# Three of eight chunks loaded transposed, and four stages of a kernel's written-out order moved by a half step

## The chip, the cores and the metric

The kernel runs on one core of one Trainium2 chip. The metric is the device time of one execution in microseconds; three runs before the change gave 368.6, 368.87 and 369.53 us, and their median, 368.87 us, is the time before.

## What is computed

For 2048 rows of 448 columns the kernel adds three things: the input, a gated long convolution, and a two-layer network with the Mish activation. Both branches take the layer-normalised input.

```python
xn = _layernorm(A_q)                                   # over the 448 columns, eps 1e-5
k_shift = sum(k_pad[:, t:t+S] * shift_k[:, 3-t] for t in range(4))
kv = k_shift * v
y = irfft(rfft(kv, 4096) * rfft(ssm_k, 4096))[:S] + kv * ssm_D
h = xn @ w1 + b1                                       # 448 -> 1792
out = A_q + xn * y + (h * tanh(softplus(h))) @ w2      # 1792 -> 448
```

## The kernel before

**The network** sets the skeleton. The rows are cut into 8 chunks of 256 (two tiles of 128, called jj), the 1792 hidden columns into 7 pairs p of 2 x 128. The program is a list of 116 slots, that is half steps, written out by `mlp_slot`: pair i = 7c + p has its first matmul stage (`g1_mm`, 22 matmuls with 256 columns) in slot 2i, its activation (`mish`) in slot 2i + 1, and its second matmul stage (`g2_mm`, 12 matmuls with 448 columns) two pairs later, in slot 2(i + 2) + 1. Every float32 operand is split in a rounded high part and a low part (XH and XL, ach and acl, w1h and w1l, w2h and w2l), and products high x high, high x low and low x high are added up.

**The layer norm** of chunk c + 1 is made while chunk c is worked on. `ln_load` brings 256 rows with rows on partitions; `bn_stats` and `bn_aggr` on DVE make mean and variance of each row, POOL makes rstd, and (x - mean) * rstd is one instruction for 128 rows on POOL (on DVE for chunks 0 and 7). DVE's share of it is put in a list (`drip`), of which `dv()` pops one entry between other DVE instructions. `g1_mm` needs the columns on partitions, so `ln_T` lets TensorE transpose each 128-row tile in four 128 x 128 blocks against an identity matrix: tile 0 in slot 14c - 3, tile 1 in slot 14c - 2, for chunk c whose first `g1_mm` is in slot 14c. The block of columns 384 to 447 is stored twice (`tail` copies 64 columns), because the fourth block carries a high and a low part in its two halves. ACT copies the transposed block out of PSUM as XH (L419), DVE subtracts for XL (L417). For chunks 5 to 7 these two are put off to the end of the slot's matmuls (`turned`, `T_LATE`).

**The convolution** is a Fourier transform in stages that are threaded through the same slots. Groups of the kernel h and of kv = (shifted k) * v are transformed by 16 packed matmuls (`f1_mm`, L125), folded on ACT and DVE (`f1_fold`) and stored to HBM scratch by DMAs from ACT's queue (`f1_out`, to Dh and Dkv, L140). `H_AT` names the slot of each h group, `KV_AT` that of each kv group; the store follows three slots later and the load five slots before. `taps` makes kv on DVE, with one product of four on POOL (`taps_pool`). From slot 63 on eight octets are read back (`o_load`: ah and av) and transformed (`h2_mm`, `v2_mm`, `prod`, `i1_mm`), and from slot 98 on `i2_mm` and `gate` finish chunk by chunk.

**What sets the order**: `at(slot, f)` puts f before the slot's network work, `after(slot, f)` behind it, and within one slot the calls run in the order in which they were registered. Each engine, and each of the DMA queues of SP, ACT and POOL, works through its own instructions in that order. Buffers: w1 and w2 pieces and k tiles share four `kr` buffers, h, v and tap tiles share seven `x` buffers, the q tiles of the chunks share three `qt` buffers, and there is one `xn`.

**The output**: `g2_evac` adds a chunk's result to its q tile, and for chunks 0 to 5 SP stores the tile at once (L494) in slot 14c + 18; the gated convolution is added to it in HBM later.

Of the kernel before, what the change touches and what calls it, by code (L numbers as in the profile page):

```python
# [7 lines left out]
F32 = mybir.dt.float32  # L8
# [7 lines left out]
NJ = 16  # L16
# [21 lines left out]
@with_exitstack  # L38
def tile_kernel(ctx: ExitStack, tc, q, k, v, sk, hT, sD, w1, b1, w2, c_f1, c_g, c_gi, c_i2, out):
    nc = tc.nc  # L40
# [24 lines left out]
    rstd = cp.tile([128, NJ], F32, name="rstd")  # L65


    w1h = wp.tile([128, 4, F], F32R, name="w1h")
# [49 lines left out]
    def f1_mm(src, g, key):  # L118
        x = src.pop(g)
        PS[key, g] = ps = [pc(), pc()]  # L120
        for b in range(2):
            for h in range(2):
                for jj in range(2):
                    rg = 32 * (2 * b + h)
                    nc.tensor.matmul(ps[h][64 * jj:64 * jj + 64, b, :D], f1[rg:rg + 32, 0:64], x[rg:rg + 32, jj],  # L125
                                     start=True, stop=True, tile_position=(rg, 64 * jj))
# [185 lines left out]
    def gate(c):  # L312
        p = PS.pop(("P", c))
        for jj in range(2):
            j = 2 * c + jj
            r = rstd[:, j:j + 1]
# [43 lines left out]

    XS, XN, turned = {}, {}, []

    def ln_load(c, eng=None):
# [3 lines left out]
        else:  # L367
            for jj in range(2):
                nc.sync.dma_start(Q[c][:, jj], q[:, jj])

    def ln_parts(c):
        st = mp.tile([128, 2, 6], F32, name="bst", bufs=2)
        ve = mp.tile([128, 2], F32, name="ve", bufs=2)
        xn = mp.tile([128, 2, D + 64], F32, name="xn", tag="xn", bufs=1)
        XN[c] = xn
        eng = nc.gpsimd if 0 < c < NCHUNK - 1 else V

        def stats(jj):
            V.bn_stats(st[:, jj], Q[c][:, jj])

        def aggr(jj):
            V.bn_aggr(mv[:, 2 * c + jj], st[:, jj])

        def eps(a, b):
            V.tensor_scalar(ve[:, a:b], mv[:, 2 * c + a:2 * c + b, 1], EPS, None, op0=ALU.add)  # L385

        def power(a, b):
            nc.gpsimd.tensor_tensor(rstd[:, 2 * c + a:2 * c + b], ve[:, a:b], mhalf[:, a:b], op=ALU.pow)  # L388

        def norm(jj):  # L390
            j = 2 * c + jj
            eng.tensor_scalar(xn[:, jj, :D], Q[c][:, jj], mv[:, j, 0:1], rstd[:, j:j + 1],  # L392
                              op0=ALU.subtract, op1=ALU.mult)

        def tail(a, b):
            eng.tensor_copy(xn[:, a:b, D:], xn[:, a:b, D - 64:D])
# [24 lines left out]
    def ln_T(c, jj):  # L421
        if jj == 0:
            dv(len(drip))
            x_tiles(c)
        p = g1p.tile([128, 2, CH], F32, name="pg1").rearrange("p a b -> p (a b)")
        transposes(c, jj, p)

        def halves():
            for lo in range(2):
                x_split(c, jj, p, lo)  # L430

        turned.append(halves)
        if c < T_LATE:
            turn()

    def turn():
        while turned:
            turned.pop()()

# [46 lines left out]
    def g2_evac(c, jjs=(0, 1)):  # L486
        x = Q[c]
        for jj in jjs:
            V.tensor_add(x[:, jj], P2.pop((c, jj))[:, :D], x[:, jj])
            dv()  # L490
            if late(c):
                nc.sync.dma_start(out[:, 2 * c + jj], x[:, jj])
        if not late(c):
            nc.sync.dma_start(out[:, 2 * c:2 * c + 2], x)  # L494

    def mlp_slot(s):
# [3 lines left out]
        if half == 0:  # L500
            if i < n:
                c, p = pairs[i]
                if c + 1 < NCHUNK:
                    if p == 0:
                        ln_load(c + 1)
                    if p == (3 if c in (0, 2, NCHUNK - 2) else 2):
                        ln_stats(c + 1)
                    if c == 0:
                        dv(len(drip))
                    if p == NP - 1:  # L510
                        ln_T(c + 1, 1)
                g1_mm(i)
        else:
            if i < n:
                c, p = pairs[i]
                if p == NP - 2 and c + 1 < NCHUNK:
                    ln_T(c + 1, 0)
# [26 lines left out]
    for g, t in enumerate(KV_AT):  # L544
# [8 lines left out]
        after(t, f1_fold, g, "kv")  # L553
        at(t + 3, f1_out, Dkv, g, "kv")

# [39 lines left out]
    wz = cp.tile([128, NJ], F32, name="wz")  # L595
    V.memset(wz, 0.0)
    ve0 = cp.tile([128, 2], F32, name="ve0")
    warm = g2p.tile([128, 512], F32, name="pg2")
    for _ in range(WARM):
        nc.tensor.matmul(warm[0:NJ, 0:WARM_N], wz, wz[:, 0:1].to_broadcast([128, WARM_N]), start=True, stop=True)  # L600

# [35 lines left out]
    for s in range(nslots):  # L637
# [7 lines left out]
        for fn, args in fns:  # L645
            if fn in (h2_out, v2_out, i1_out):
                fn(*args)
        turn()
        for fn, args in fns:
# [6 lines left out]
def _constants():  # L656
# [19 lines left out]
    for kk in range(64):  # L676
# [8 lines left out]
    c = lambda a: np.ascontiguousarray(a, dtype=np.float32)  # L685
    return dict(c_f1=c(np.stack([f1, np.eye(128)], axis=1)), c_g=c(G.reshape(128, 8, 4, 2, 32)), c_gi=c(GI.reshape(128, 8, 2, 2, 64)),
                c_i2=c(i2))
# [27 lines left out]
```

## Time and profile before

| what | value |
|---|---|
| median of 3 runs | 368.87 us |
| the profiled execution's own time | 370.86 us |
| its span from first to last instruction | 368.9 us |
| TensorE clock granted | full, in all 40 slices |
| DVE busy | 262.5 us, 71% |
| ACT busy | 166.3 us, 45% |
| POOL busy | 71.2 us, 19% |
| moved by DMA | 79.35 MB |

The span and the 1.96 us around it make up the profiled execution. PE stands for TensorE's matmuls, PEld for its weight loads, DVE for VectorE, ACT for ScalarE, POOL for GpSimd; SPq, ACTq and POOLq are the queues from which these engines issue DMAs. A row of the timeline has start and duration in us, engine, line, operation, tiles written and read, shapes, a count, and in brackets the idle time before it with what ended it. Several matmuls are in flight at once, so the distance from one start to the next is a matmul's cost, and its duration is not.

### The profile page before, as it was taken

How to read it: one execution, taken by the hardware profiler on the slowest of the kernel's cores; microseconds unless marked ns; L12 is line 12 of the kernel's file. 1: busy time of each engine (PE TensorE's matmuls, PEld its weight loads, DVE VectorE, ACT ScalarE, POOL GpSimd, SP SyncE). 2: the span in 40 equal slices, each digit the busy share in tenths (PEclk: the TensorE clock that was granted, in tenths of full speed). 3: DMA queues.
4: the chain of work that ended last, by engine and by line, in shares of the span. 5: the costliest groups of instructions: out<-in, count | busy, mean ns of one | idle time of the engine just before them, and what ended most of it. 6: DMA issues, size and time to landing. Idle time of an engine off the chain costs nothing.

```text
span 368.9 us, 7464 instructions
## 1 busy us (share of the span) xinstructions
PE 360.9 (98%) x3128; PEld 292.6 (79%) x3128; DVE 262.5 (71%) x359; ACT 166.3 (45%) x277; POOL 71.2 (19%) x58
## 2 busy tenths in 40 slices
PE   7998999999999999999999999999999999999995
PEld 2697888978888989889868666666666889889885
DVE  5897858999998888996515657656385752897751
ACT  3757543344241443253254555556655533235450
POOL 2005000920228222611006000060000005102020
PEclk9999999999999999999999999999999999999999
DMA  7998996839496329514675598896694375949655
GB/s 241 346 285 312 358 368 184 256 105 295 105 299 214 89 66 274 170 48 101 225 244 174 194 261 238 282 301 189 209 292 125 95 248 205 419 195 276 116 66 133
DMA packets 32354, 79.35 MB, mean 215 GB/s; under 512 B 2881, under 2 KB 19138, under 8 KB 32322
## 3 DMA queue, kind: packets, MB, share of 16 engines
q1 hardware_dynamic: 20210, 44.09, 35.8%
q10 hardware_dynamic: 9776, 22.88, 22.2%
q0 software_dynamic: 2336, 11.93, 11.3%
q8 instruction: 24, 0.39, 0.4%
q14 instruction: 8, 0.07, 0.1%
HBM read 50.44 MB, written 28.44 MB: 214 GB/s over the span
## 4 chain that ended last, share of the span: by engine, by line
PE 71%; DMA 12%; DVE 9%; POOL 3%; ACT 2%; issue 2%; SPq 0%; ACTq 0%; POOLq 0%; DVEq 0%
PE pg L457 27%; PE pg L482 10%; PE pg L484 9%; PE pg L483 9%; PE pc L208 7%; DMA kr<-in_w_dram 6%; PE pc L251 4%; PE pc L125 2%; PE pc L308 2%; DMA Dh<-st 2%; DVE x L172 2%; PE pg L407 2%; POOL xn L392 2%; DMA Dkv<-st 1%; DMA av<-Dkv 1%
## 5 line engine op out<-in xcount | busy, mean ns | idle before, releaser
L465 ACT ACTIVATE a<-pg,b1t 128x256 f32<-128x256 f32 x112 | 47.1, 472 | 113.0 <-PE pg L457 88.2
L457 PE MATMUL pg<-XH,w1h 128*128 128x256 f32 x448 | 91.3, 285 | 0.9 <-ACT XH L419 0.9
L75 DVE TENSOR_TENSOR acl<-a,ach 128x512 fp32r<-128x512 f32 x56 | 38.8, 693 | 65.0 <-ACT ach L74 64.7
L457 PEld LDWEIGHTS pg<-XH,w1h 128*128 128x128 f32 x448 | 69.6, 188 | 18.9 <-issue 15.7
L482 PE MATMUL pg<-w2h,ach 128*128 128x448 f32 x224 | 83.1, 371 | 0.0
L483 PE MATMUL pg<-w2l,ach 128*128 128x448 f32 x224 | 81.3, 363 | 0.9 <-DVE w2l L75 0.9
L484 PE MATMUL pg<-w2h,acl 128*128 128x448 f32 x224 | 81.4, 363 | 0.0
L457 PE MATMUL pg<-XL,w1h 128*128 128x256 f32 x448 | 69.6, 277 | 0.2 <-DVE XL L417 0.2
L457 PEld LDWEIGHTS pg<-XL,w1h 128*128 128x128 f32 x448 | 59.4, 188 | 0.4 <-DVE XL L417 0.4
L457 PE MATMUL pg<-XH,w1l 128*128 128x256 f32 x336 | 56.8, 277 | 0.0
L482 PEld LDWEIGHTS pg<-w2h,ach 128*128 128x128 f32 x224 | 42.0, 188 | 11.7 <-issue 9.4
L457 PEld LDWEIGHTS pg<-XH,w1l 128*128 128x128 f32 x336 | 46.8, 188 | 0.0
L483 PEld LDWEIGHTS pg<-w2l,ach 128*128 128x128 f32 x224 | 42.1, 188 | 3.6 <-DVE w2l L75 1.2
L484 PEld LDWEIGHTS pg<-w2h,acl 128*128 128x128 f32 x224 | 42.1, 188 | 2.5
L388 POOL TENSOR_TENSOR rstd<-ve,mhalf 128x2 f32<-128x2 f32 (+1 forms) x9 | 8.8, 977 | 156.2 <-DVE ve L385 156.1
L74 ACT CAST ach<-a 128x512 fp32r<-128x512 f32 x56 | 34.7, 620 | 1.8
L155 POOL TENSOR_TENSOR x<-kr,skb 128x896 f32<-128x896 f32 x8 | 17.1, 2133 | 83.6 <-DVE x L154 62.4
L392 POOL TENSOR_SCALAR xn<-qt,mv,rstd 128x448 f32<-128x448 f32 x12 | 27.8, 2320 | 0.6
L172 DVE TENSOR_TENSOR x<-x 128x896 f32<-128x896 f32 x24 | 26.8, 1115 | 1.4 <-POOL x L155 0.9
L131 ACT COPY st<-pc 128x896 f32<-128x896 f32 x16 | 14.5, 906 | 14.5 <-PE pc L125 12.6
L132 DVE TENSOR_TENSOR st<-pc,st 128x896 f32<-128x896 f32 x16 | 17.4, 1088 | 3.6 <-ACT st L131 3.1
L259 ACT COPY qe<-pc 128x896 f32<-128x896 f32 x16 | 13.8, 912 | 11.0 <-PE pc L251 10.8
(70 smaller groups left out, 389.7 us busy)
## 6 DMA issues: line engine op xcount, KB each, us to landing
Dh<-st ACTq DMA_DIRECT2D x16, 448.0 KB, 6.4
Dkv<-st ACTq DMA_DIRECT2D x16, 448.0 KB, 5.1
ah<-Dh SPq DMA_DIRECT2D x8, 896.0 KB, 7.0
av<-Dkv SPq DMA_DIRECT2D x8, 896.0 KB, 6.2
E<-qe ACTq DMA_DIRECT2D x16, 448.0 KB, 5.2
e<-E POOLq DMA_DIRECT2D x8, 896.0 KB, 7.9
kr<-in_k_dram SPq DMA_DIRECT2D x10, 448.0 KB, 6.7
x<-in_v_dram SPq DMA_DIRECT2D x8, 448.0 KB, 5.2
```

What stands on the lines that cost most here:

```text
L74: nc.scalar.copy(h, raw)
L75: V.tensor_sub(l, raw, h)
L132: V.tensor_add(st[:, 0], e, st[:, 1])
L155: nc.gpsimd.tensor_mul(o, KR[g - u // 2], skb[:, u:u + 1].to_broadcast([128, 2, D]))
L172: V.tensor_add(KV[g], KV[g], o)
L208: nc.tensor.matmul(p[32 * t:32 * t + 32, r, :D], g[rs, t, c], a[rs, t], start=True, stop=True, tile_position=(64 * r, 32 * t))
L392: eng.tensor_scalar(xn[:, jj, :D], Q[c][:, jj], mv[:, j, 0:1], rstd[:, j:j + 1], op0=ALU.subtract, op1=ALU.mult)
L457: nc.tensor.matmul(ps[:, n], l, r, start=n_ == 0, stop=n_ == len(mm) - 1)
L465: nc.scalar.activation(a[:, n], ps[:, n], AF.Mish, bias=b1t[:, 2 * p + n:2 * p + n + 1])
L482: nc.tensor.matmul(ps, ah[:, n, cs], w2h[:, f], start=f == 0, stop=False)
L483: nc.tensor.matmul(ps, ah[:, n, cs], w2l[:, f], start=False, stop=False)
L484: nc.tensor.matmul(ps, al[:, n, cs], w2h[:, f], start=False, stop=f == NF - 1)
```

## The change

For chunks 5, 6 and 7 (`NT = 5`) the host supplies q a second time, already transposed (`qT`: 128 partitions, four column blocks, 256 rows, the last block repeated in part). It is loaded straight into the `xn` buffer. Mean and variance still come from the rows-on-partitions tile. Since each row now is a column, mean and rstd have to be the same on all partitions: POOL stores the 256 pairs (mean, rstd) to a scratch row in HBM (`nt_store`), SP reads half of that row back to all 128 partitions (`nt_row`, once for each jj), and DVE subtracts and multiplies in place (`nt_norm`, two instructions with 512 elements a partition for each jj). ACT and DVE then make XH and XL from SBUF (`nt_split`). The tile for the row takes over the identity matrix's space. No transposes are made for these chunks. The slots are written relative to b = 14(c - 1).

Besides: h groups 3, 0, 4 and 5, their loads and stores move one slot later, and `POOL_H` from 20 to 21. The output stores of chunks 0 to 5 move to the end of the slot after. For chunks 1 to 4 the `tail` copy of tile 0 runs before the norm of tile 1. The last kv store moves from slot 63 to 62, the first octet's ah load from the start of slot 61 to the end of slot 60. The constants f1 and identity become two loads, f1 (half as wide) last in ACT's first loads.

```diff
-H_AT = {2: 4, 3: 8, 0: 12, 4: 16, 5: 20, 6: 26, 7: 32}
+H_AT = {2: 4, 3: 9, 0: 13, 4: 17, 5: 21, 6: 26, 7: 32}
-POOL_H = {20: (0, 2)}
+POOL_H = {21: (0, 2)}
-T_LATE = 5
+NT = 5
+NT_AT = {"q": -5, "x": -1, "stats": -2, "flush": 0, "row": (4, 8), "norm": (7, 10), "split": (8, 11)}
...
+    MR = {c: dp.tile([2, CH], F32, name="MR") for c in range(NT, NCHUNK)}
-    f1id = cp.tile([128, 2, 128], F32, name="f1id")
-    f1, ident = f1id[:, 0], f1id[:, 1]
+    f1 = cp.tile([128, 64], F32, name="f1")
+    idr = cp.tile([128, CH], F32, name="idr")
+    ident = idr[:, 0:128]
...
-                     lambda: [f(*a) for f, *a in ((power, 0, 2), (norm, 0), (norm, 1), (tail, 0, 2))]])
+                     lambda: [f(*a) for f, *a in ((power, 0, 2), (norm, 0), (tail, 0, 1), (norm, 1), (tail, 1, 2))]])
+
+    def xT_load(c):
+        XN[c] = xn_tile()
+        nc.sync.dma_start(XN[c], qT[c])
+
+    def nt_stats(c):
+        stats, aggr, eps, power, norm, tail = ln_parts(c)
+        drip.extend([lambda: stats(0), lambda: stats(1), lambda: aggr(0), lambda: aggr(1),
+                     lambda: (eps(0, 2), power(0, 2), nt_store(c))])
+
+    def nt_store(c):
+        nc.gpsimd.dma_start(MR[c].rearrange("j (p t) -> p j t", t=2), mv[:, 2 * c:2 * c + 2])
+
+    def nt_row(c, jj):
+        nc.sync.dma_start(idr, MR[c][jj].partition_broadcast(128))
+
+    def nt_norm(c, jj):
+        x = XN[c][:, :, 128 * jj:128 * jj + 128]
+        for t, op in enumerate((ALU.subtract, ALU.mult)):
+            m = idr.rearrange("p (a t) -> p t a", t=2)[:, t:t + 1].to_broadcast([128, 4, 128])
+            V.tensor_tensor(x, x, m, op=op)
+            dv()
+
+    def nt_split(c, jj):
+        if jj == 0:
+            x_tiles(c)
+        x, h, l = (t[:, :, 128 * jj:128 * jj + 128] for t in (XN[c], *XS[c]))
+        nc.scalar.copy(h, x)
+        V.tensor_sub(l, x, h)
+        dv()
...
-        if not late(c):
-            nc.sync.dma_start(out[:, 2 * c:2 * c + 2], x)
+
+    def g2_out(c):
+        nc.sync.dma_start(out[:, 2 * c:2 * c + 2], Q[c])
...
-        at(t + 3, f1_out, Dkv, g, "kv")
+        at(t + (3 if g < NO - 1 else 2), f1_out, Dkv, g, "kv")
...
-        at(h - d if o else h - 2, o_load, AH, Dh, o, "ah")
+        (at if o else after)(h - d if o else h - 3, o_load, AH, Dh, o, "ah")
...
+    for c in range(NT, NCHUNK):
+        b = 2 * NP * (c - 1)
+        at(b + NT_AT["q"], ln_load, c)
+        at(b + NT_AT["x"], xT_load, c)
+        at(b + NT_AT["stats"], nt_stats, c)
+        at(b + NT_AT["flush"], lambda: dv(len(drip)))
+        for jj in range(2):
+            at(b + NT_AT["row"][jj], nt_row, c, jj)
+            after(b + NT_AT["norm"][jj], nt_norm, c, jj)
+            after(b + NT_AT["split"][jj], nt_split, c, jj)
...
+    for c in range(NCHUNK - LATE):
+        after(2 * (NP * (c + 1) + G2_LAG) + 1, g2_out, c)
...
-    nc.scalar.dma_start(f1id, c_f1)
+    nc.scalar.dma_start(ident, c_id)
...
+    nc.scalar.dma_start(f1, c_f1)
```

More of the change, by code (lines that the diff above doesn't have):

```diff
@@ L38, in tile_kernel @@
 @with_exitstack
-def tile_kernel(ctx: ExitStack, tc, q, k, v, sk, hT, sD, w1, b1, w2, c_f1, c_g, c_gi, c_i2, out):
+def tile_kernel(ctx: ExitStack, tc, q, qT, k, v, sk, hT, sD, w1, b1, w2, c_f1, c_id, c_g, c_gi, c_i2, out):
     nc = tc.nc
@@ L65, in tile_kernel, with rs @@
     rstd = cp.tile([128, NJ], F32, name="rstd")
+    def rs(c):
+        return rstd[:, 2 * c:2 * c + 2] if c < NT else mv[:, 2 * c:2 * c + 2, 1]
     w1h = wp.tile([128, 4, F], F32R, name="w1h")
@@ L315, in gate @@
             j = 2 * c + jj
[L316 removed]
+            r = rs(c)[:, jj:jj + 1]
             x = (Q if late(c) else QA)[c][:, jj]
@@ L369, in ln_load, with xn_tile @@
                 nc.sync.dma_start(Q[c][:, jj], q[:, jj])
+    def xn_tile():
+        return mp.tile([128, 4, CH], F32, name="xn", bufs=1)
     def ln_parts(c):
@@ L373, in ln_parts @@
         ve = mp.tile([128, 2], F32, name="ve", bufs=2)
-        xn = mp.tile([128, 2, D + 64], F32, name="xn", tag="xn", bufs=1)
-        XN[c] = xn
+        if c < NT:
+            XN[c] = xn = xn_tile().rearrange("p a b -> p (a b)").rearrange("p (j d) -> p j d", j=2)
         eng = nc.gpsimd if 0 < c < NCHUNK - 1 else V
@@ L426, in ln_T @@
         transposes(c, jj, p)
[L428 to L438, printed above, removed]
+        for lo in range(2):
+            x_split(c, jj, p, lo)
     AHL, P1, P2 = {}, {}, {}
@@ L502, in mlp_slot @@
                 c, p = pairs[i]
-                if c + 1 < NCHUNK:
+                if c + 1 < NT:
                     if p == 0:
                         ln_load(c + 1)
-                    if p == (3 if c in (0, 2, NCHUNK - 2) else 2):
+                    if p == (3 if c in (0, 2) else 2):
                         ln_stats(c + 1)
@@ L515, in mlp_slot @@
                 c, p = pairs[i]
-                if p == NP - 2 and c + 1 < NCHUNK:
+                if p == NP - 2 and c + 1 < NT:
                     ln_T(c + 1, 0)
@@ L594, in tile_kernel @@
     V.memset(one, 1.0)
-    wz = cp.tile([128, NJ], F32, name="wz")
+    wz = cp.tile([128, 8], F32, name="wz")
     V.memset(wz, 0.0)
@@ L599, in tile_kernel @@
     for _ in range(WARM):
-        nc.tensor.matmul(warm[0:NJ, 0:WARM_N], wz, wz[:, 0:1].to_broadcast([128, WARM_N]), start=True, stop=True)
+        nc.tensor.matmul(warm[0:8, 0:WARM_N], wz, wz[:, 0:1].to_broadcast([128, WARM_N]), start=True, stop=True)
     nc.scalar.activation(ve0, mhalf, AF.Mish)
@@ L696 @@
     lay = lambda x: x.reshape(32, 2, 2, 16, D).transpose(2, 1, 0, 3, 4).reshape(128, NJ, D)
+    rows = np.concatenate([np.arange(D), np.arange(384, D)]).reshape(4, 128)
+    turn = lambda x: x.reshape(128, NCHUNK, 2, D)[..., rows].transpose(1, 4, 3, 2, 0).reshape(NCHUNK, 128, 4, CH)
     kpad = np.pad(a["A_k"][0], ((4, 0), (0, 0)))
     arrs = dict(
-        q=lay(a["A_q"][0]), k=np.concatenate([lay(kpad[:S])[:, :, :][:, :4], lay(a["A_k"][0])], axis=1),
+        q=lay(a["A_q"][0]), qT=turn(lay(a["A_q"][0])), k=np.concatenate([lay(kpad[:S])[:, :, :][:, :4], lay(a["A_k"][0])], axis=1),
         v=lay(a["A_v"][0]), sk=a["A_shift_k"].T, hT=lay(a["A_ssm_k"].T), sD=a["A_ssm_D"][None],
```

11 lines of the change are left out of this document (5 added, 6 removed).

## The prediction

> **What bounds the kernel now.** First the page's busy line and the windows, to see which engine fills which stage.
>
> ```profile
> PE 360.9 (98%) x3128; PEld 292.6 (79%) x3128; DVE 262.5 (71%) x359; ACT 166.3 (45%) x277; POOL 71.2 (19%) x58
> ```
>
> ```profile
> 30.00:40.00 10.00, 9.06 (x62) 8.39 (x61) 9.12 (x12) 7.79 (x13) 3.77 (x3) 1.00 0.89 299
> 60.00:80.00 20.00, 20.00 (x155) 17.46 (x154) 18.57 (x28) 8.05 (x15) 10.99 (x6) 1.00 0.70 209
> 80.00:100.00 20.00, 20.00 (x166) 16.72 (x165) 19.57 (x27) 7.61 (x14) 2.14 (x1) 1.00 0.63 184
> 100.00:120.00 20.00, 19.71 (x156) 17.16 (x155) 18.85 (x27) 5.70 (x11) 9.91 (x5) 1.00 0.81 257
> 180.00:200.00 20.00, 19.66 (x196) 15.47 (x195) 7.00 (x11) 8.61 (x17) 5.83 (x4) 1.00 0.76 251
> 220.00:240.00 20.00, 20.00 (x234) 12.82 (x233) 12.50 (x16) 10.39 (x15) 0.00 (x0) 1.00 0.87 266
> ```
>
> Columns are the stretch, its length, then busy us of PE, PEld, DVE, ACT and POOL, the granted clock (1.00 throughout), DMA share and GB/s. PE is full except in three windows. So the time is TensorE's own work plus a few short stalls, and a cut pays in full only if it shortens PE's sequence or one of those stalls. From 60 to 120 us DVE is a second bound: 57 of 60 us busy. After 180 us DVE has room (7.5 us idle of 20 at 220 to 240).
>
> Then the timeline, for the three stalls. At 31 us:
>
> ```profile
> 31.45 0.47 PE L482 MATMUL pg<-w2h,ach 128*128 128x448 f32 x1
> 32.87 0.47 PE L483 MATMUL pg<-w2l,ach 128*128 128x448 f32 x1 [0.94 <-DVE w2l L75]
> 33.18 0.36 PE L484 MATMUL pg<-w2h,acl 128*128 128x448 f32 x1
> 33.38 0.36 PE L482 MATMUL pg<-w2h,ach 128*128 128x448 f32 x1
> ```
>
> Undisturbed 448-column matmuls start 0.20 apart (33.18 to 33.38); this pair is 1.42 apart, so 1.2 us are lost. The chain of waits tells why:
>
> ```profile
> 20.06 8.35 DMA kr<-in_w_dram
> 28.44 0.58 ACTq L140
> ...
> 31.43 1.39 DVE w2l L75
> 32.87 0.47 PE pg L483
> ```
>
> ACT's queue stood at the issue of an h store (L140) until a w2 load had landed, though the store does not read that tile. Behind it ACT's activation and the split of w2 came late. I infer that the two transfers share a completion semaphore.
>
> At 118 us and 191 us:
>
> ```profile
> 118.39 0.55 PE L407 MATMUL pg<-f1id,xn 128*128 128x128 f32 x3
> 119.23 0.33 PE L407 MATMUL pg<-f1id,xn 128*128 128x128 f32 x1 [0.29 <-POOL xn L396]
> 119.31 0.45 PE L482 MATMUL pg<-w2h,ach 128*128 128x448 f32 x1
> ```
>
> ```profile
> 112.89 5.69 POOL xn L392 x2
> 118.64 0.55 POOL xn L396
> ```
>
> ```profile
> 191.70 1.33 PE L208 MATMUL pc<-av,g 64*32 64x448 f32 x20 [0.34 <-DMA av<-Dkv]
> ```
>
> Chunk 3's transposes wait for a tail copy that stands behind both norms on POOL (2.85 us each). The first v2 stage waits 0.34 us for the last kv group's way through HBM.
>
> **The change part by part.**
>
> **Transposes of chunks 5 to 7 (24).** Chunk 7's first four, and the same passage one pair later without them:
>
> ```profile
> 309.54 0.62 PE L457 MATMUL pg<-XL,w1h 128*128 128x256 f32 x4
> 310.00 0.60 PE L407 MATMUL pg<-f1id,xn 128*128 128x128 f32 x4
> 310.35 0.45 PE L482 MATMUL pg<-w2h,ach 128*128 128x448 f32 x1
> 310.64 0.37 PE L483 MATMUL pg<-w2l,ach 128*128 128x448 f32 x1
> ...
> 315.41 0.63 PE L457 MATMUL pg<-XL,w1h 128*128 128x256 f32 x4
> 315.88 0.37 PE L482 MATMUL pg<-w2h,ach 128*128 128x448 f32 x1
> 316.09 0.36 PE L483 MATMUL pg<-w2l,ach 128*128 128x448 f32 x1
> ```
>
> From the last x4 group to L483 it is 1.10 us with transposes and 0.68 without: 0.42 for four. Chunk 5's, behind packed matmuls, start 0.41 before the next stage:
>
> ```profile
> 200.15 0.65 PE L407 MATMUL pg<-f1id,xn 128*128 128x128 f32 x4
> 200.56 0.45 PE L482 MATMUL pg<-w2h,ach 128*128 128x448 f32 x1
> ```
>
> Six groups of four by 0.42 are **2.5 us** off PE's sequence. The other bound is the busy time of all 64:
>
> ```profile
> L407 PE MATMUL pg<-f1id,xn 128*128 128x128 f32 x64 | 10.3, 281 | 0.8 <-DVE xn L392 0.4 <-POOL xn L396 0.3
> ```
>
> 10.3 / 64 x 24 = 3.9 us, but these spans overlap their neighbours; I keep 2.5, the distance between starts.
>
> The mean here is 281 ns. The Trainium skill ("TensorE: Matmul & The Clock Gate", Part 4: PE-mode transpose) gives about 275 ns for one in a kernel, most of it access latency. The trace agrees on the duration; but counted one after another, 24 would be 6.6 us by that figure, and the starts here, about 0.1 us apart, do not bear that out.
>
> **What replaces them**: for each chunk a 512 KB load and two 128 KB row loads on SP, a store of 256 pairs on POOL, four DVE instructions with 512 elements, and the high and low parts as before, only from SBUF. Nearest rows for DVE and for a landing:
>
> ```profile
> L75 DVE TENSOR_TENSOR acl<-a,ach 128x512 fp32r<-128x512 f32 x56 | 38.8, 693 | 65.0 <-ACT ach L74 64.7
> q<-in_q_dram POOLq DMA_DIRECT2D x3, 448.0 KB, 10.2
> ```
>
> 4 x 0.69 = 2.8 us of DVE for a chunk, at slots 14c - 7 and 14c - 4, against 7.5 us idle in 20: hidden, and 0 in the sum. If that cover is gone, 3 x 2.8 = 8.4 us of DVE come late, with `prod` and acl behind them. POOL loses four norms and DVE two; none of these ended a wait of PE. A row is issued at slot b + 4 (b + 8) and used behind b + 7 (b + 10). For chunk 6 that first stretch begins at 231.27 and ends behind 246.94:
>
> ```profile
> 231.27 2.71 PE pg L457 x22
> ...
> 246.94 1.69 PE pc L251 x32
> ```
>
> 15.7 us over four slots; the second has three, 11.8 us at the same pace. The slowest kind of load here takes 10.2, in the row above. The row load waits on SP for the store's landing, and the second one for the first norm on DVE; behind it in SP's queue stand av and ah loads, which PE waits for, and which themselves wait for the PE stage of the same slots. Cost 0; the other end is the slow rival below. Extra DMA, 2.3 MB in all at 266 GB/s, is 9 us of transfer beside the octets' loads: 0 again, bounded by the 0.34 us stall at 191 us in each of eight octets, 2.7.
>
> **Chunk 3's tail**: the first transposes now wait for one norm and one tail, about 112.89 + 2.85 + 0.4 = 116.1, before 118.39. Without the stall the four cost 0.35 (310.00 to 310.35) in place of 0.92: **0.5 us** gained, at worst 0 if the second norm becomes late (its tail ends near 119.4, needed at 121).
>
> **The start**: `ident` alone is 64 KB in place of 128 KB ahead of w1 on ACT's queue. 64 KB at the first slice's 241 GB/s are 0.27 us; **0.2 us** gained, between 0 and 0.27. f1 comes last on that queue and is needed at slot 1; at worst it lands late by its own 32 KB, 0.1 us.
>
> **h groups one slot later**: the work on PE is the same. On SP the w2 and w1 loads of slots 3 and 7 now go ahead of two h loads, and all transfers behind pair up differently with the stores on ACT. The stall of 1.2 us at 31 us can go entirely or stay, or strike another slot; I take **0.8 us** gained, nearer to the full end because the w2 loads come earlier.
>
> One thing speaks against it. `taps(0, 2)` is registered behind slot 24 - 7 + 3 = 20, and `taps_pool(0, 2)` now behind slot 21. So DVE makes this product itself, and POOL's comes afterwards and is used by nobody. Its price is one
>
> ```profile
> L162 DVE TENSOR_TENSOR x<-kr,skb 128x896 f32<-128x896 f32 x8 | 8.8, 1096 | 1.7 <-DMA kr<-in_k_dram 1.7
> ```
>
> that is 1.1 us where DVE idles 1.4 us of 20 (60 to 80). If PE now arrives a microsecond earlier, DVE there is what sets the pace. I take **0.6 us** given back, between 0 and 1.4 (all gains before 60 us, 0.2 + 1.2).
>
> **Last kv store and stats of chunk 5**:
>
> ```profile
> 179.01 0.53 DVE bst L379
> ...
> 180.53 0.55 DVE bst L379
> ...
> 181.17 5.38 DMA Dkv<-st
> 186.64 4.93 DMA av<-Dkv
> ```
>
> Two bn_stats lie on the way to this store. Chunk 5's are now flushed by slot 56, so the way is up to 1.1 us shorter and the stall of **0.3 us** goes (bounds 0 and 0.34).
>
> **Output stores later on SP**: nothing on PE reads them, and a q tile's next load comes at least four slots behind; 0. They no longer hold the loads queued behind them, which were on time anyway.
>
> **Sum**: -2.5 - 0.5 - 0.2 - 0.8 + 0.6 - 0.3 = -3.7 us. The profiled execution took 370.86 (span 368.9 and 1.96 around it) and would take 367.2, 2.0 above the median of the runs shown; applied to that median, 368.87 - 3.7 = **365.2 us**.
>
> **The rivals.**
>
> **A, transposes alone.** The stall at 31 us moves to another slot and DVE between 60 and 120 us takes back what else was gained before it. For it: DVE is busy 57 of those 60 us. Against it: DVE's work is itself released slot by slot, so it moves forward with PE. -2.5 + 0.9 (dead product and a stalled kv stage) gives -1.6: **367.3 us**.
>
> **B, the change does not do what it says on PE.** XH and XL of a chunk come no earlier than the first `g1_mm`, which then waits about as long as the eight transposes took. For it: ACT and DVE work in order and the splits stand behind octet work. Against it: the last split is behind slot 14c - 3, two slots ahead, 5 us or more. -2.5 + 2.5 - 0.5 + 0.6: about **369.0 us**.
>
> **C, slower: the row's way through HBM.** 256 stores of 8 bytes, their completion, then 128 reads of one row. If the second row of a chunk takes over 11.8 us, DVE stands at `nt_norm` in order, and `prod`, acl and the low part stand behind it. For it: no load here has such a shape, and the second row waits for the first norm. Against it: 128 KB is little beside the 448 KB that took 10.2 us. At 16 us the first row is just in time and the second 4.2 us late, 12.6 us in three chunks; half of it hidden in DVE's idle time, 6 us are added: 365.2 + 6 = **371 us**. It decides, as slower by 0.3%, from about 15 us on.
>
> The Trainium skill ("DMA: Bandwidth & Descriptors", Specifications) wants 512 bytes or more in a transfer and says that below that the engines read, modify and write. By this rule the store is the slowest kind here. No run yet shows such a store, and the only time it would change is C's.
>
> **How the numbers follow.** The forecast 0.62, A 0.17, B 0.08, C 0.13. A measurement of this kernel (368.6 to 369.53) tells about 0.3% from no change, that is 367.8 to 370.0. The forecast's own range is 364.1 (-2.5 - 0.5 - 0.2 - 1.2 - 0.34, nothing given back) to 366.5 (half of the small gains). Half of the way to the 3.9 bound of the transposes takes the low end to 363.4; over A and B, with 0.4 for the octets' loads, the high end is 369.4. C is left out. Faster: the forecast and most of A, 0.76. Same: B and a little of A, 0.11. Slower: C, 0.13.
>
> **What would show it.** Right: no L407-like transposes behind 165 us, PE starting a new stage with no gap near 200, 262 and 310 us; no wait of L483 for w2l; none for the tail copy at 118; PE full in the windows 220 to 320. The dead product: POOL still has eight tap products while DVE has one 896-wide product more. Wrong: idle time of DVE ended by the row load, XH or XL as releaser of PE at the start of chunks 5 to 7, or a stall for f1's x tiles between 60 and 120 us, which would mean that DVE takes the gains back.

## The result, and the profile after

The changed kernel took 370.91 us (median of 12 runs, 369.81 to 372.28) beside 369.42 for the kernel before (12 runs): a ratio of 1.0043, interval 1.0027 to 1.006. It is slower by 0.4%, 1.5 us, where 365.2 us and a gain of 3.7 were forecast. The profiled execution took 371.19 (span 369.4). A second set of 10 runs gave 371.3, ratio 1.0053 (1.0032 to 1.0074). In some runs the mean granted clock was 0.991 to 0.997, and where a profile caught this (e6, e11) it was 0.83 from 10 to 20 us, and pairs 0 to 13 took 1.6 us longer (73.2 us in e6, 71.6 in e2).

The busy line of the changed kernel's page:

```profile
PE 360.6 (98%) x3104; PEld 291.2 (79%) x3104; DVE 271.7 (74%) x369; ACT 166.4 (45%) x277; POOL 66.4 (18%) x59
```

Its windows (length of the stretch, then PE, PEld, DVE, ACT and POOL busy, granted clock, DMA share and GB/s):

```profile
20.00:30.00 10.00, 9.07 (x61) 8.49 (x61) 8.72 (x15) 8.28 (x12) 0.65 (x1) 1.00 1.00 324
...
60.00:80.00 20.00, 19.97 (x152) 17.37 (x151) 19.44 (x28) 7.62 (x15) 9.85 (x7) 1.00 0.67 207
80.00:100.00 20.00, 19.60 (x151) 15.98 (x157) 19.55 (x25) 7.12 (x13) 4.05 (x2) 1.00 0.71 211
180.00:200.00 20.00, 18.75 (x169) 15.71 (x168) 9.43 (x12) 8.33 (x14) 0.00 (x0) 1.00 0.82 256
```

PE has 24 matmuls fewer and is not done earlier. Three windows show idle time: 0.93 at 20 to 30 (before: 0.94 at 30 to 40), 0.40 at 80 to 100 (before: none) and 1.25 at 180 to 200 (before: 0.34). DVE is busy 9.2 us longer; from 60 to 80 it has 0.56 us to spare, before 1.43.

The timeline of the changed kernel's PE at the places that the prediction named, and at one that it did not (start, duration, engine, line, tiles, in brackets the idle time):

```profile
25.11 0.36 PE L511 MATMUL pg<-w2h,ach 128*128 128x448 f32 x1
26.40 0.48 PE L512 MATMUL pg<-w2l,ach 128*128 128x448 f32 x1 [0.93 <-DVE w2l L81]
...
80.76 0.97 PE L131 MATMUL pc<-x,f 32*64 32x448 f32 x4
81.91 1.00 PE L131 MATMUL pc<-x,f 32*64 32x448 f32 x12 [0.19 <-DVE st L140]
82.84 0.66 PE L446 MATMUL pg<-idr,xn 128*128 128x128 f32 x4
...
120.33 0.66 PE L446 MATMUL pg<-idr,xn 128*128 128x128 f32 x4
120.75 0.45 PE L511 MATMUL pg<-w2h,ach 128*128 128x448 f32 x1
...
160.79 0.60 PE L446 MATMUL pg<-idr,xn 128*128 128x128 f32 x4
161.57 0.39 PE L486 MATMUL pg<-XH,w1h 128*128 128x256 f32 x1 [0.18 <-DVE XL L456]
...
194.58 1.74 PE L214 MATMUL pc<-av,g 64*32 64x448 f32 x32 [1.23 <-DMA av<-Dkv]
...
200.81 0.62 PE L486 MATMUL pg<-XL,w1h 128*128 128x256 f32 x4
201.36 0.98 PE L214 MATMUL pc<-ah,g 64*32 64x448 f32 x16
...
311.11 0.62 PE L486 MATMUL pg<-XL,w1h 128*128 128x256 f32 x4
311.56 0.36 PE L511 MATMUL pg<-w2h,ach 128*128 128x448 f32 x1
```

The transposes are gone from 165 us on, and the next stage follows at once (201.36, 311.56). The wait for w2l has not gone but stands at 26.40. A convolution stage at 80.76, which takes 0.94 us undisturbed, takes 2.08, because DVE is late with a fold (L140). Chunk 3's stall behind the tail copy is gone (120.33 to 120.75), and chunk 4's first `g1_mm` has a new wait for XL (161.57). The wait for av has grown from 0.34 to 1.23.

Where the time lies can be read from the starts of the `g1_mm` stages (the first of 22 matmuls at L486, at L457 before) in the timelines. Distances in us; "again" is a second profile of the same kernel:

| kernel | pair 0 to 13 | 13 to 20 | 20 to 28 | 28 to 33 | 33 to 34 | 34 to 48 | 48 to 55 |
|---|---|---|---|---|---|---|---|
| before | 72.99 | 40.39 | 43.77 | 29.94 | 9.35 | 107.98 | 41.91 |
| before again | 71.45 | 40.37 | 43.94 | 29.78 | 9.35 | 107.98 | 41.91 |
| changed | 75.04 | 39.89 | 44.14 | 31.02 | 8.54 | 106.66 | 41.75 |
| changed again | 75.37 | 39.99 | 44.16 | 30.83 | 8.56 | 106.42 | 41.74 |
| e10, before with the later h groups | 72.14 | 41.03 | 43.95 | 29.74 | 9.34 | 108.05 | 41.91 |
| e2, changed with h as before | 71.60 | 39.97 | 44.14 | 30.93 | 8.55 | 107.77 | 41.75 |
| e9 again, transposed loads alone | 71.90 | 40.36 | 43.69 | 29.87 | 8.62 | 106.74 | 41.75 |
| e12, e9 with one constant load | 71.56 | 40.36 | 43.69 | 30.04 | 8.56 | 106.75 | 41.75 |

The last three columns hold chunks 5 to 7: the transposes bring 2.5 us by the second profile of the changed kernel (0.79 + 1.56 + 0.17) and 2.1 by e9's (0.73 + 1.24 + 0.16). E2's 107.77 holds a wait of 1.24 us for hs at 229.96, behind two stores of E whose issues held ACT's queue for 4.02 us; no other profile has more than 0.25 there. The first column loses 2 to 4 us, the fourth 1.1. Which edit does that is the question of the experiments.

### The profile page after: what moved, and what is told of

It is laid out like the page before. It is cut to its first block, busy times and chain, and to the rows that moved or that the text cites. A ratio compares the mean times of both kernels' runs of the same rounds, so it can differ in the third digit from the quotient of the medians.

```text
span 369.4 us, 7451 instructions
## 1 busy us (share of the span) xinstructions
PE 360.6 (98%) x3104; PEld 291.2 (79%) x3104; DVE 271.7 (74%) x369; ACT 166.4 (45%) x277; POOL 66.4 (18%) x59
## 4 chain that ended last, share of the span: by engine, by line
PE 50%; DMA 3%; DVE 2%; ACT 1%; ACTq 1%; issue 0%; SPq 0%
PE pg L486 19%; PE pg L511 7%; PE pc L214 6%; PE pg L513 6%; PE pg L512 6%; PE pc L257 4%; PE pc L314 2%; DMA Dkv<-st 2%; DMA av<-Dkv 1%; ACTq L268 1%; DVE x L178 1%; PE pc L131 1%; ACT a L494 0%; DVE x L181 0%; ACT qe L265 0%
## 5 line engine op out<-in xcount | busy, mean ns | idle before, releaser
L486 PE MATMUL pg<-XH,w1h 128*128 128x256 f32 x448 | 91.0, 285 | 1.4 <-ACT XH L458 1.1
L486 PEld LDWEIGHTS pg<-XH,w1h 128*128 128x128 f32 x448 | 69.9, 188 | 19.4 <-issue 15.1
L486 PE MATMUL pg<-XL,w1h 128*128 128x256 f32 x448 | 69.7, 277 | 0.2 <-DVE XL L456 0.2
L486 PEld LDWEIGHTS pg<-XL,w1h 128*128 128x128 f32 x448 | 59.4, 188 | 0.4 <-DVE XL L456 0.4
L486 PE MATMUL pg<-XH,w1l 128*128 128x256 f32 x336 | 56.8, 278 | 0.0
L486 PEld LDWEIGHTS pg<-XH,w1l 128*128 128x128 f32 x336 | 46.9, 188 | 0.0
L178 DVE TENSOR_TENSOR x<-x 128x896 f32<-128x896 f32 x24 | 26.3, 1097 | 2.7 <-POOL x L161 2.0
L161 POOL TENSOR_TENSOR x<-kr,skb 128x896 f32<-128x896 f32 x8 | 17.9, 2236 | 52.4 <-DVE x L160 30.6
L397 POOL TENSOR_TENSOR mv<-ve,mhalf 128x2 f32<-128x2 f32 x3 | 2.9, 969 | 99.3 <-DVE ve L394 99.2
L401 POOL TENSOR_SCALAR xn<-qt,mv,rstd 128x448 f32<-128x448 f32 x8 | 19.1, 2387 | 0.4
L397 POOL TENSOR_TENSOR rstd<-ve,mhalf 128x2 f32<-128x2 f32 (+1 forms) x6 | 6.9, 1158 | 68.0 <-DVE ve L394 59.2
```

What stands on the lines that cost most here:

```text
L161: nc.gpsimd.tensor_mul(o, KR[g - u // 2], skb[:, u:u + 1].to_broadcast([128, 2, D]))
L178: V.tensor_add(KV[g], KV[g], o)
L486: nc.tensor.matmul(ps[:, n], l, r, start=n_ == 0, stop=n_ == len(mm) - 1)
```

## The experiments

The kernels that ran together share the runs of the kernel before. Ratios are to that kernel, with their interval.

**Is it the unused product, or the later groups?** `e1_live_product` brings POOL's product back ahead of DVE's, so that it is used, and keeps the groups later; `e2_h_as_before` takes both back.

```diff
-POOL_H = {21: (0, 2)}
+POOL_H = {20: (0, 2)}
...
-        if t in POOL_H:
-            after(t, taps_pool, *POOL_H[t])
+        if t - 1 in POOL_H:
+            after(t - 1, taps_pool, *POOL_H[t - 1])
```

> The changed kernel with POOL's tap product of kv group 0 put back behind slot 20, ahead of its use, so that DVE uses it and makes none of its own; the h groups stay one slot later. Theory D (dead product): in the changed kernel POOL runs this product at 72.9 to 76.0 us for nobody, DVE's multiply beside it takes 2.99 us in place of 1.10, and the fold behind it holds PE by 1.14 us at the f1 stage at 80.8 and by 0.5 us at the transposes behind it. Then that multiply takes 1.1 us again, the f1 stage at 81 us takes 0.94 in place of 2.08, and the time is 1.5 to 2.5 us below the changed kernel's 370.9: 368.4 to 369.4, ratio to before 0.997 to 1.000. Rival H (the later h groups themselves): the folds of h are late whoever makes the product; then the stall at 81 us stays above 0.8 us and the time stays above 370.2. Rival V (the last kv group's way through HBM): the largest single stall is at 194 us, 1.4 us; it does not change here, and alone it would leave 370.0 or more.

```diff
-H_AT = {2: 4, 3: 9, 0: 13, 4: 17, 5: 21, 6: 26, 7: 32}
+H_AT = {2: 4, 3: 8, 0: 12, 4: 16, 5: 20, 6: 26, 7: 32}
-POOL_H = {21: (0, 2)}
+POOL_H = {20: (0, 2)}
```

> The changed kernel with all h groups and POOL's product in the slots of before (8, 12, 16, 20). Theory D: as far as kv group 0 is concerned the same as with the product alive, so 368.4 to 369.4; the stall at 25 us for w2l (1.1 us, in the second g2 stage) then shows whether the later h loads moved it: if it goes back to 31 us or vanishes, the h loads' place sets it, if it stays at 25 us, the split of the two constants does. Rival H: the whole loss of the changed kernel is here, 368.0 or less (0.8% below the changed kernel). Rival V: 370 or more.

`e1_live_product` took 370.6 us (ratio 1.0029, 1.0012 to 1.0045), 0.3 below the changed kernel; `e2_h_as_before` 369.46 (0.9994, 0.9972 to 1.0015), 1.45 below it. So the later groups cost, and not the unused product alone. The timeline of DVE, first of e1, then of e2, shows how:

```profile
68.20 1.09 DVE L178 TENSOR_TENSOR x<-x 128x896 f32<-128x896 f32 x1 [2.04 <-POOL x L161]
69.21 0.69 DVE L81 TENSOR_TENSOR acl<-a,ach 128x512 fp32r<-128x512 f32 x1
69.81 1.08 DVE L138 TENSOR_TENSOR st<-pc,st 128x896 f32<-128x896 f32 x1
70.93 1.09 DVE L140 TENSOR_TENSOR st<-pc,st 128x896 f32<-128x896 f32 x1
```

```profile
63.95 1.09 DVE L138 TENSOR_TENSOR st<-pc,st 128x896 f32<-128x896 f32 x1 [1.09 <-ACT st L137]
64.96 0.16 DVE L394 TENSOR_SCALAR ve<-mv 128x2 f32<-128x2 f32 x1
65.08 1.09 DVE L140 TENSOR_TENSOR st<-pc,st 128x896 f32<-128x896 f32 x1
66.09 1.08 DVE L178 TENSOR_TENSOR x<-x 128x896 f32<-128x896 f32 x1
```

With the groups as before, DVE folds h group 5 (L138, L140) while POOL makes its product, and idles 1.09. One slot later the fold stands behind the sum (L178) that needs the product: DVE idles 2.04 us and then has the fold still to do, in the stretch in which it has hardly any time to spare. PE shows it a little later, in the timeline of e1 and then of e2:

```profile
75.86 1.01 PE L131 MATMUL pc<-x,f 32*64 32x448 f32 x16 [0.53 <-DVE x L181]
```

```profile
72.87 1.01 PE L131 MATMUL pc<-x,f 32*64 32x448 f32 x16
```

In the changed kernel DVE makes the product itself and idles only 0.31 us before the fold. POOL's product comes later and meets another instruction of DVE. Its DVE, then its POOL timeline:

```profile
72.92 1.09 DVE L181 TENSOR_TENSOR x<-x 128x896 f32<-128x896 f32 x1
73.93 2.99 DVE L168 TENSOR_TENSOR x<-kr,skb 128x896 f32<-128x896 f32 x1
```

```profile
72.94 3.03 POOL L161 TENSOR_TENSOR x<-kr,skb 128x896 f32<-128x896 f32 x1
79.82 2.11 POOL L161 TENSOR_TENSOR x<-kr,skb 128x896 f32<-128x896 f32 x1 [3.85 <-DVE x L160]
```

The product of DVE that the prediction priced at 1.1 us took 1.06 (at 64.84). The next one like it (L168 above) ran beside POOL's, now unused, product and took 2.99. So DVE has some 3 us more to do here, and behind it works without a pause up to the fold that PE waits for at 81.91. The medians of the changed kernel and e1 are only 0.3 us apart: the same edit costs about as much by a longer DVE here as by an idle one there.

**The later groups in the kernel before.**

```diff
-H_AT = {2: 4, 3: 8, 0: 12, 4: 16, 5: 20, 6: 26, 7: 32}
+H_AT = {2: 4, 3: 9, 0: 13, 4: 17, 5: 21, 6: 26, 7: 32}
...
+        if t - 1 in POOL_H:
+            after(t - 1, taps_pool, *POOL_H[t - 1])
```

> The kernel before with h groups 3, 0, 4 and 5, their loads and stores one slot later, POOL's product staying behind slot 20, and nothing else of the change. Theory H: the later groups alone cost what the changed kernel loses by its pair 13 (3.0 us in its profile against the kernel with the groups as before): a stall of 1.1 us or more for w2l in the second g2 stage at 25 us, and 0.5 to 1 us for kv group 0 near 73 us; 1 to 2.5 us above before: 370.3 to 371.8. Rival C (the two constants loaded apart, one load more at the start): without that load there is no stall at 25 us, and the time is 369.3 to 369.9.

370.87 us, ratio 1.0044 (1.0027 to 1.0062): this edit by itself, with the product used, makes the kernel before slower by 1.6 us. In the table, 0.7 of it lies ahead of pair 13 and 0.65 between 13 and 20, where PE waits 0.94 us for chunk 3's tail copy on POOL at 118.85 (0.28 in the second profile of before).

**Does the order of the loads make it?** `e11_h_loads_early` is e1 with the loads of h back in their old slots.

```diff
-            at(t - 5 if t > 7 else t - 3, h_load, g)
+            at(t - 6 if g in (3, 0, 4, 5) else t - 5, h_load, g)
```

> The changed kernel with POOL's product alive (370.6), and the loads of h groups 3, 0, 4 and 5 back in their slots of before; transforms and stores stay one slot later. Theory B (two issues at once): in the changed kernel SP issues the load of h group 3 at 18.3 us beside ACT's h store at 17.7, and both issues take 1.7 to 2.3 us in place of 0.4 to 0.6, which makes ACT, the w2 split and the second g2 stage late. With the load at 11 us the store's issue takes 0.6 us, the stall of 1.2 to 1.7 us at 25 us goes, and the time falls to 369.0 to 369.6. Rival F (the later fold): the stall at 25 us stays, the time stays above 370.2.

370.85 us (1.0027, 1.0006 to 1.0048): no gain on e1. Its profile has no stall for w2l, which e1's has (1.41 us before 27.44), but DVE's 2.04 us behind POOL's product and PE's 0.53 behind it are as in e1. The order of the h loads is not what costs most.

**The kernel before and the changed kernel once more**, for what recurs.

> The kernel before once more, for a second profile. The profiled execution of before took 370.86, 1.4 us above its median of 369.42. If its stalls at 31 us (1.2), 118 us (0.5) and 191 us (0.34) are of the kernel, all three return here within 0.3 us; if they are of that execution, some are gone and the span is some 367.5.

> The changed kernel once more, for a second profile. Of the kernel, and so here again within 0.4 us: the stall at the f1 stage near 81 us (1.1, with 0.5 at the transposes behind it), the wait for av near 191 us (1.4), chunk 4's wait for XL near 161 us (0.4). Of that execution, and so perhaps gone: the 1.2 us for w2l at 25 us.

The second profile of the kernel before took 369.66 us and has no stall for w2l at all; the waits for the tail copy (0.28) and for av (0.17) are there. The changed kernel again has the w2l stall (0.86 at 26.74), the late fold and the av wait (1.12). So the stall of 1.2 us at 31 us, which the prediction set out to gain, belonged to one execution. There the w2 load for which ACT's queue waits landed 8.36 us after its issue, in the second profile 6.58; that the h store waits for the load's semaphore, as the prediction inferred, stands in the trace (number 104 for both). In the changed kernel's stall ACT's queue is held in another way, by the issue itself, as the ACT timelines of the changed kernel and of e9's second profile show:

```profile
17.04 0.61 ACTq L146 DMA_DIRECT2D Dh<-st  x1
...
17.70 2.27 ACTq L146 DMA_DIRECT2D Dh<-st  x1
20.01 1.05 ACT L346 CAST w1h<-kr 128x1024 fp32r<-128x1024 f32 x1 [1.51 <-issue]
```

```profile
17.60 0.62 ACTq L147 DMA_DIRECT2D Dh<-st  x1
...
18.25 0.63 ACTq L147 DMA_DIRECT2D Dh<-st  x1
18.92 1.05 ACT L347 CAST w1h<-kr 128x1024 fp32r<-128x1024 f32 x1
```

The same issue took 2.27 us or 0.63, and e9's first profile, of the same kernel as the second, has an issue of 2.26 us and the stall (1.48 before 27.89). The changed kernel's second profile and e1 have it too (1.69 and 2.24); in the other profiles the issue takes 0.62 to 0.66. Of 110 runs of the kernel before beside the experiments, 88 lie between 368.37 and 369.87 and 22 between 370.19 and 371.33. The profiled execution of before, 370.86, is like the 22, the second one, 369.66, like the 88. That the stall makes the two groups is likely, and one profile of each doesn't show it.

**Transposed loads alone.** `e3_transposed_loads_only` takes back h, the tail copy, the output stores, the last kv store and the ah load; `e9_loads_only_rows_behind_av` is e3 with chunk 5's rows issued behind av.

```diff
-                     lambda: [f(*a) for f, *a in ((power, 0, 2), (norm, 0), (tail, 0, 1), (norm, 1), (tail, 1, 2))]])
+                     lambda: [f(*a) for f, *a in ((power, 0, 2), (norm, 0), (norm, 1), (tail, 0, 2))]])
...
-        at(t + (3 if g < NO - 1 else 2), f1_out, Dkv, g, "kv")
+        at(t + 3, f1_out, Dkv, g, "kv")
-        (at if o else after)(h - d if o else h - 3, o_load, AH, Dh, o, "ah")
+        at(h - d if o else h - 2, o_load, AH, Dh, o, "ah")
```

> The kernel before with chunks 5 to 7 loaded transposed and the two constants loaded apart, and nothing else of the change: h groups, output stores, tail copies, last kv store and first ah load as before. If the transposes' 2.5 us on PE are gained and nothing is lost elsewhere: 366.9 (before 369.4), ratio 0.993. Theory V (contention before the first v2 stage: the row load and the store of 256 pairs cost the ah and av loads their time): the v2 stage at 190 us waits 1 us or more as in the changed kernel, so 368 or more. Theory S (stores): if the wait there is 0.5 us or less, the output store, now issued between the ah load and the last kv store, is what took the time in the changed kernel.

372.07 us, ratio 1.0073 (1.0045 to 1.0101), six runs from 369.25 to 373.63, four of them with the lower granted clock; the two others took 369.25 and 371.41. So the median says little about the edit. In its PE timeline the first octet's other load is late; the row load of chunk 5 goes out just ahead of it on SP, and it lands 8.36 us after its issue (6.23 and 6.46 in e9's profiles, without the row ahead):

```profile
185.91 1.74 PE L214 MATMUL pc<-ah,g 64*32 64x448 f32 x32 [2.43 <-DMA ah<-Dh]
```

The profiled execution, with this wait, was its fastest run.

```diff
+NT_LATE = {"row": (8, 10), "norm": (9, 11), "split": (10, 12)}
...
+        T = NT_LATE if c == 5 else NT_AT
...
```

> Transposed loads for chunks 5 to 7 and nothing else of the change (h groups, output stores, tail copies, last kv store and first ah load as before), with chunk 5's two row loads moved behind the av load, to slots 64 and 66. Theory Q (order in SP's queue): with the row load ahead of ah the first h2 stage waited 2.6 us (transposed loads only), with ah ahead and the output store behind it the v2 stage waited 1.2 to 1.7 us in all five kernels that have that order. Here ah stands where it stood before, the row behind av: h2 waits nothing, v2 0.4 us as before, and the transposes' 2.5 us are left: 367 to 367.8 against 369.3 of before, ratio 0.994 to 0.996. Rival L (the extra transfers cost wherever they stand): one of the two waits stays above 1 us, time 368.3 or more.

> The kernel with only the transposed loads and chunk 5's rows behind the av load, once more, for a second profile. If the 1.9 us for w2l at 26 us belong to that execution, they are gone here, and the span is some 365.5 in place of 367.7.

e9 took 368.38 us (0.9973, 0.9954 to 0.9992): faster than the kernel before. Its second profile took 366.92.

**What makes av late: the rows or the order of the queue?** Four kernels. `e5_from_chunk6` is e2 with `NT = 6`, `e6_rows_behind_av` e2 with the rows of chunk 5 as in e9, `e7_no_rows_chunk5` e2 without them (DVE fills the unused half of that tile with zeros instead), and `e8_own_rows_chunk5` has each partition read its own 1 KB in place of the common row.

> The h groups as before, the rest of the change, but only chunks 6 and 7 loaded transposed; chunk 5 goes through TensorE again. Theory R (row loads of chunk 5): its two row loads stand among the transfers on which the first ah and av loads depend; without them the v2 stage at 188 us waits 0.4 us as in the kernel before, not 1.4, and the time falls although the eight transposes cost 0.8 us again: 368.0 to 369.0 against 369.5 with chunk 5. Rival S (output store and earlier ah load): the wait for av stays at 1.2 us or more, and with 0.8 us of transposes the time rises to 370.3.

> The h groups as before, the rest of the change with all three chunks, but chunk 5's two row loads moved from slots 60 and 64 to 64 and 66, behind the av load, its norms and splits two slots and one slot later. Theory R: the wait for av at 188 us falls to 0.4 us, nothing new waits since chunk 5's first matmul is at slot 70; 368.0 to 368.7, that is 0.8 to 1.4 us below the 369.5 with the rows in their place, and the runs spread less than its 367.4 to 371.1. Rival S: the wait for av stays at 1.2 us or more, time 369.5. A new wait is possible: ACT as releaser of PE (XH, L440) near 213 us, for the second row has only some 10 us.

```diff
-        nc.sync.dma_start(idr, MR[c][jj].partition_broadcast(128))
+        if c > NT:
+            nc.sync.dma_start(idr, MR[c][jj].partition_broadcast(128))
...
+    after(60, lambda: V.memset(idr[:, 128:], 0.0))
```

> The h groups as before and the rest of the change, without the two row loads of chunk 5: its subtraction and product work on the identity matrix and zeros, so that part of the output is not the reference's. Theory R: the wait for av falls to 0.4 us, time 368.0 to 368.7. Rival S: it stays at 1.2 us or more.

```diff
-        nc.sync.dma_start(idr, MR[c][jj].partition_broadcast(128))
+        nc.sync.dma_start(idr, q[:, jj, 0:CH] if c == NT else MR[c][jj].partition_broadcast(128))
```

> The h groups as before and the rest of the change; chunk 5's two row loads bring the same 128 KB each, but every partition its own 1 KB of q in place of one row read 128 times, so chunk 5 is normalised with the wrong numbers. In the changed kernel the 256 packets of 1024 bytes between 170 and 192 us (row and g) took 171 ns each on average, in the kernel before the 128 of g alone 77 ns. If the one row read 128 times is what is slow, these packets fall to about 80 ns, 1.3 us of all engines are free again, and the wait for av falls by half a microsecond or more against 1.4; if the bytes and the place in the queue count, it stays within 0.3 us of 1.4.

370.68 (1.0032, 1.0012 to 1.0052), 369.43 (0.9984, 0.9966 to 1.0002), 368.71 (0.9974, 0.9954 to 0.9995) and 369.16 us (0.9983, 0.9961 to 1.0006). The av wait stays in all four: 1.05, 1.16, 1.48 and 1.14. So in this order of the queue the rows do not make it. In e9 it is 0.18. The chain of waits, first of the changed kernel, then of e9, and SP's queue in the same order:

```profile
178.76 2.73 PE pg L486 x22
...
181.52 0.85 ACT a L494 x2
...
183.06 6.46 DMA Dkv<-st
189.53 0.02 SPq L201
...
189.59 4.85 DMA av<-Dkv
```

```profile
182.36 5.38 DMA Dkv<-st
...
187.81 4.78 DMA av<-Dkv
```

```profile
177.31 0.42 SPq L201 DMA_DIRECT2D ah<-Dh  x1
178.77 0.35 SPq L524 DMA_DIRECT2D out_dram<-qt  x1
189.59 0.37 SPq L201 DMA_DIRECT2D av<-Dkv  x1
```

```profile
178.07 0.34 SPq L524 DMA_DIRECT2D out_dram<-qt  x1
178.50 0.38 SPq L199 DMA_DIRECT2D g<-in_c_g_dram  x1
178.94 0.64 SPq L202 DMA_DIRECT2D ah<-Dh  x1
187.81 0.37 SPq L202 DMA_DIRECT2D av<-Dkv  x1
```

Av waits for the last kv store. In the six profiles with the output store ahead of ah (both of before, e10, both of e9, e12) that store lands 5.38 to 5.53 us after its issue; in the nine with the output store behind ah (both of the changed kernel, e1, e2, e5 to e8, e11) it takes 6.23 to 6.60. The 1.0 us between the two means is most of the fourth column's loss. In the sixteenth profile, e3, with the row load between the output store and ah, it takes 7.85.

Why it lands later stays open. That it shares the DMA engines with the output store and ah is not the whole of it: in e5 to e8 those two have left the engines by the time the store moves. The DMA view shows it, from the store's issue to its landing (packets, MB, share of 16 engines; q10 is ACT's queue, q1 SP's), first of e9's second profile, 179.8 to 185.2 us, then of e5, 180.5 to 186.8:

```profile
q10 hardware_dynamic: 288, 0.92, 52.4%
q1 hardware_dynamic: 384, 0.66, 31.8%
```

```profile
q10 hardware_dynamic: 288, 0.92, 61.7%
```

In e5 SP's queue moves nothing, and the store still takes longer: the 256 packets of 3584 bytes, of this store and the one just before it, take 242 ns each on average (242 to 244 in e5 to e8) against 176 in e9's second profile. Which part of the edit does it, the output store's place, the earlier ah load or the earlier kv store, was not tried apart.

**One load for f1 and the identity**, on e9.

```diff
-    f1 = cp.tile([128, 64], F32, name="f1")
-    idr = cp.tile([128, CH], F32, name="idr")
-    ident = idr[:, 0:128]
+    f1id = cp.tile([128, 2, 128], F32, name="f1id")
+    f1, ident = f1id[:, 0, 0:64], f1id[:, 1]
+    idr = f1id.rearrange("p a b -> p (a b)")
...
-    nc.scalar.dma_start(ident, c_id)
+    nc.scalar.dma_start(f1id, c_f1)
...
-    nc.scalar.dma_start(f1, c_f1)
```

> As the kernel with only the transposed loads and chunk 5's rows behind the av load (368.4), but f1 and identity come in one load again, as in the kernel before, and that one tile takes the rows after its last use. Theory P (the first microseconds): the load more at the start is what makes the stall for w2l near 26 us (2 us in that kernel's profile) frequent; without it the time falls by 0.5 us or more, to 367.9 or less, ratio 0.996 or less, and the profile has no stall above 0.6 us between 20 and 35 us. Rival N (it comes and goes with the execution in every kernel): the time stays within 0.4 us of 368.4.

367.0 us (12 runs, 366.23 to 369.32), ratio 0.9946 (0.9925 to 0.9967): the fastest kernel here, 2.1 below the 369.08 of before beside it. Against e9 it is 1.4 us, though the two intervals overlap a little. No profile shows where: e9's second profile, without a w2l stall, has a span of 365.1, e12's 365.7. What e12 may do is make the executions with that stall rarer (10 of its 12 runs lie below 368.0, of e9's 12 five), and that was not followed further. Without the two of e9's runs that had the lower granted clock, e9's median is 367.98 and the difference 1.0.

## Why the prediction was wrong

**Transposes: right.** Named as 2.5 us and measured as 2.1 to 2.5 (table). The sum of starts was the right reading, the busy time (3.9) the wrong one. What replaces them was hidden as forecast: DVE's `nt_norm` took 8.3 us in all, as estimated, and rival C did not come about; that the measured 370.91 lies at C's 371 is chance. The landings of the store and the rows, as the changed kernel's view of their tile has them (least, median, most):

```profile
DMA to landing us min/median/max: 3.0/6.3/9.0
```

None reaches the 11.8 us that were to decide. Of the rule that the Trainium skill gives for transfers below 512 bytes ("DMA: Bandwidth & Descriptors", Specifications) nothing is to be seen in the time: in e2 the 256 pairs of chunk 5 went out as 16 packets of 128 bytes, 58 ns each.

**Later h groups: the step that failed first.** The prediction took them as -0.8 + 0.6, measured are +1.45 (changed kernel against e2) and +1.6 (e10). The -0.8 came from reading a stall of one execution as the kernel's, and it was taken off a median, 368.87, that lay 2.0 us below that execution. In both profiles of the changed kernel a stall for w2l is there. The +0.6 was the right worry, DVE between 60 and 80 us, with too small a size: it priced the one instruction that DVE gains (1.06) and not the next one, which ran beside POOL's unused product and took 1.9 us longer than its median. With the product used (e1, e10) the move costs as much in another way: the fold of a group filled DVE's wait for POOL's product, and the prediction treated its move as free because PE's work was the same.

**Last kv store: -0.3 forecast, about +1.0 measured** (368.38 for e9 against 369.43 for e6, which differ in the queue order and the tail copy). The two bn_stats named were indeed on the chain before, but PE's `g1_mm` and ACT's activation, which stand on the changed kernel's chain above, ended just as late: the store starts 7.4 us ahead of pair 32 with them and 7.5 without (181.17 and 188.6 before, 183.06 and 190.6 after). And "output stores later: 0" asked who reads the stores and not whether their new place changes the landing of the one transfer that PE waits for. It came on average 1.0 us later in the nine profiles with the new order, and by which way is open.

**Chunk 3's tail: -0.5 forecast, 0 measured.** The stall went, 0.4 us by the second column (40.36 to 39.97), and 0.45 came back in the third (43.69 to 44.14), where chunk 4's XL is late behind POOL's norms and product (161.57). The bound "at worst 0 if the second norm becomes late" had the right end, at another chunk.

**Start: -0.2 forecast, perhaps +1.0 to 1.4** (e9 against e12). The prediction counted bytes ahead of w1, and the edit adds a load. That this is the whole of the 1.4 us is not shown.

Together: -2.5 + 1.45 + 1.0 + 0 + 1.4 = +1.35 us, against 1.5 measured. These terms come from medians that each hold within some 0.8 us. The three costs are the steps from e12 over e9 and e6 or e2 to the changed kernel, so they add up to its distance from e12 by themselves; what the sum checks is 2.5 against the 2.1 by which e12 is ahead of before. No rival of the prediction was this: rival A took DVE's stretch to give back the small gains, 0.9 at most, and the actual cost there was larger than all of these. A's mechanism came about in part: a stall for w2l stands at another slot, and DVE takes time back. The upper end of the forecast's own range does not follow from its terms: half of the small gains of 1.8 us, with 0.6 given back, makes 366.1 and not 366.5; nothing hangs on it.

## What to carry to other kernels

Before a stall is counted as a gain, look for it in a second profile: here it was there in some executions and not in others. Moving work that "costs the same" changes what covers a wait: on an engine that is full, list what it does while it waits for another engine, and see whether the moved work was that. When transfers change places, follow the one whose landing PE waits for, and compare its landing in profiles of both orders; which transfers it shares the engines with did not tell it here.

## What the hardware showed that was not expected

A row that was read as soon as it was stored was slow to read. Chunk 7's first row load has 128 packets of 1 KB, with no other load of such packets beside it. In the nine profiles where SP issues it within 0.03 us of the landing of POOL's store, they take 93 to 281 ns on average (263 in the changed kernel's first profile); in the four where it goes out 11 us or more behind the landing (e3, both of e9, e12), 46 to 55. That one row is read by all 128 partitions does not make it slow by itself; what does is not shown.

A store that has the DMA engines to itself was no faster: the packets of the last two kv stores took 242 to 244 ns in e5 to e8, with nothing of SP's queue beside them, and 167 to 183 in the six profiles where part of ah's load was still moving.

The issue of a DMA on ACT's queue took 0.6 us or 2.27, for the same store at the same place, with ACT idle behind it.

DVE's product of 896 elements (L168) took 2.99 us beside POOL's product, which itself took 3.03 instead of 2.11; the median of its nine is 1.08. The ends look as if the two took turns: DVE's L181 ends at 74.01, POOL's product 1.96 later at 75.97, L168 0.95 behind that at 76.92. That is an inference from one place.
